# Order of the work between the pair loop and the first tile, and of the last stores, in a Hyena filter with a maxout FFN

## The chip, the core and the metric

The kernel runs on one core of a Trainium2 chip: TensorE (PE, matrix products into PSUM), VectorE (DVE), ScalarE (ACT), GpSimd (POOL) and SyncE (SP), each with its own instruction stream, and 16 DMA engines that serve transfers issued by SP, ACT and POOL. The metric is the device time of one execution in microseconds. Several executions give a median; one more is taken with the hardware profiler, and its trace gives the times inside.

## The reference

A long convolution (done with a Fourier transform) of u = x v with a filter that comes from a small MLP, a product with x, and a maxout FFN on the result:

```python
def _attn_ref(x, v, pos_emb, w1, w2):            # x, v: (4, 12544, 128)
    h_mlp = np.maximum(pos_emb @ w1, 0.0) @ w2
    window = np.exp(-0.01 * np.arange(S))[:, None]
    h_filt = h_mlp * window
    u = x * v
    L = 2 * S
    Uf = np.fft.rfft(u, n=L, axis=1)
    Hf = np.fft.rfft(h_filt, n=L, axis=0)
    y = np.fft.irfft(Uf * Hf[None, :, :], n=L, axis=1)[:, :S, :]
    return x * y

def _moe_ref(x, w1, w2, w3, w_out):              # x: (50176, 128), w1..w3: (128, 768)
    h = np.maximum(np.maximum(x @ w1, x @ w2), x @ w3)
    return h @ w_out
```

All arrays are float32.

## The kernel before

**The transform.** The 12544 positions of a batch entry are cut as 98 blocks (n) of 128 phases (p). The transform over n gives 90 frequencies, handled as 45 pairs (NK = 45); the transform over p, with its twiddle factors, is a product with a 128x128 matrix for each frequency. The input is taken in 32 units of 4 rows of 4 channels: a unit is loaded (`u_load`), multiplied (`u_mul`), turned with PE (`u_turn`), transformed over n (`u_products`) and written into `spec` in SBUF. `u_products` returns three further steps: `top`, a copy by ACT; `sums`, four DVE operations; `fours`, four more. `u_first` does all at once.

**The pair loop** (from line 1171) makes, for batch entry 0 and for each pair g: the filter's spectrum; the forward products `g_second`; the product with the spectrum (`g_re`, `g_im`); the sums `ab` of `g_unfold`; and the inverse products `g_third`, three pairs later. `g_third` copies its PSUM bank to `zs` with ACT, and SP stores `zs` to `zd` in HBM. The last pair's zs is copied besides to a small HBM tensor `ze` (two rows for each half c), by SP and by ACT. The matrices of `g_third` are loaded by `load_dir(s, 1)` on SP, three pairs ahead, into three buffers; the call stands behind that of `g_third`, so behind the store to `zd` on SP.

**The tiles.** A tile is 4 phases x 98 blocks, 392 positions; there are 32 for each batch entry. `t_load` reads its 90 rows from zd into `zt` (rows by frequency, halves c of 45 rows). For the first tile, POOL loads 44 rows of each half from zd, and SP the last row of each half from ze; POOL loads x for tiles 0 and 1 (`x_load`, four DMAs of 98 KB) ahead of zt. `t_sums` makes sum and difference of zt's halves. `t_last` multiplies them by a 90x98 table (32 matmuls over the four phases, s = 0 to 3), and DVE multiplies by x, which gives `gt`. Then come the FFN's steps. `up` makes hid = max(relu(gt (w2 - w1)), gt (w3 - w1)) for 128 of the 768 columns: two products into banks of `hps` (three banks, in turn), a relu by ACT, a max by DVE. `down` multiplies by w_out and adds up in a bank of `ops`, together with gt times `lin` = w1 w_out.

**The passage** (lines 1209 to 1234 and 1267 to 1284), by hand, between loop and tiles: units 0 and 1 of batch entry 1 (`u_first`), the last two `g_third` (pairs 43 and 44), six `folding` steps that make `lin` (a transpose of 128 columns of w1, an ACT copy `w1t`, a product into `pl`), the turning of units 4 and 5, the products of units 2, 3 and 4, and the first tile's sums and `t_last`. Each step needs PSUM banks: `cps` has three of tag "cv", `gps` two (g0, g1), `sps` two of tag "h" and one, `pl`. When the loop's pools are closed, the tiles' pools take the same banks.

**The rest.** While the tiles of one batch entry run, a planner (`conv_steps`) spreads the next entry's transform over them. The last entry's tiles are taken in pairs with an FFN of fewer products (`products`, `ORDER`); its results c11, c12, c21 and c22 are quarters of the output of two tiles (first digit: tile; second: half m of the output columns), kept in one buffer for each m, and `stored(m)` writes both of a buffer: for the last two tiles with one DMA on SP and one on ACT for each quarter. In the plan, c21 is followed by `stored(0)`, and c12, the last one, by `stored(1)`.

Each engine runs its instructions in the order in which they are written down here; the waits between engines are put in by the framework from the buffers read and written.

Of the kernel before, what the change touches and what calls it, by code (L numbers as in the profile page):

```python
# [16 lines left out]
P = 128  # L17
GC = 4
# [77 lines left out]
def kernel(  # L96
# [32 lines left out]
    zd = [dram.tile([N1, 2, 64, 256] if b == 0 else [N1, 2, 32, 2, 256], FP32, name=f"zd{b}")  # L129
          for b in range(B)]  # L130

    ze = dram.tile([2, 2, 2, 256], FP32, name="ze")

    f1_t, f1e_t, f1h_t, f4p_t, w_t, wq_t = tables(NB)
    f1_d = nc.inline_tensor(f1_t, name="f1_const").ap()
# [512 lines left out]
                                    op=op)  # L648
        abs_[g] = ab

    def g_third(g):
        w, ab = ws.pop((g, 1)), abs_.pop(g)
        ps = state["cv"][1].tile([P, 512], FP32, tag="cv", name="ps3")
        for k in range(2):
            for q in range(2):
                halves_mm(ps[:, (2 * k + q) * D:(2 * k + q + 1) * D], w[:, k, q, :],
                          ab[:, k, q, :], k == 0 and q == 0, True)
        if g < NK - 2:
            zs = state["cv"][0].tile([P, 2, 256], FP32, tag="z", name="zs", bufs=2)
        else:  # L660
            zs = lwp.tile([P, 2, 256], FP32, tag="w1", name="zs")
        nc.scalar.copy(zs[:].rearrange("p k f -> p (k f)"), ps[:])
        if g == NK - 1:
            for c in range(2):
                (nc.scalar if c else nc.sync).dma_start(ze[c], zs[64 * c:64 * c + 2])
        nc.sync.dma_start(
            zd[0][2 * g:2 * g + 2].rearrange("k c t f -> (c t) k f"), zs[:])

# [105 lines left out]
    def x_load(b, i, eng):  # L774
# [3 lines left out]
                          x[:, 4 * i:4 * i + 8, c, b, :])  # L778
        xTs[b, i], xTs[b, i + 1] = xT[:, 0], xT[:, 1]

    def t_load(b, i):
        if b == i == 0:
            x_load(b, i, nc.gpsimd)
        zt = hp.tile([N1, 2, 512], FP32, tag="zt", name="zt", bufs=2)
        for c in range(2):
            if b == 0:
                n = NK if i else NK - 1
                (nc.sync if i else nc.gpsimd).dma_start(
                    zt[NK * c:NK * c + n],
                    zd[b].rearrange("(g a) c t f -> g a c t f", a=2)[  # L790
                        0:n, :, c, 2 * i:2 * i + 2, :].rearrange("g a t f -> g a (t f)"))
                if i == 0:
                    nc.sync.dma_start(
                        zt[NK * c + n:NK * c + NK].rearrange("o a (t f) -> o a t f", t=2),
                        ze[c:c + 1].rearrange("o t a f -> o a t f"))
                continue
            q, j = divmod(i, NT // 2)
            for a in range(2):
                nc.sync.dma_start(
                    zt[NK * c:NK * c + NK, a].rearrange("g (t f) -> g t f", t=2),  # L800
                    zd[b].rearrange("(g a) c t q f -> g a c t q f", a=2)[
                        :, a, c ^ (a & q), 2 * j:2 * j + 2, q, :])
        zts[b, i] = zt[:, 0], zt[:, 1]
        if i % 2 == 0 and (b or i > 2):
            x_load(b, i, nc.gpsimd if 0 < i < NT - 2 and b < B - 1 else nc.sync)

# [94 lines left out]
    def products(b, i, h, X, Y):  # L901

        m1, m2 = lin[:, 0:64], lin[:, 64:128]
        first, second_ = gs[b, i], gs[b, i + 1]
        t = {}

        def new(name, bufs=1):
            return lp.tile([P, H2], FP32, tag=name, name=name, bufs=bufs)

        def mm(ps, w, rhs, start):  # L910
            for q in range(4):
                c, m = divmod(32 * q, 64)
                nc.tensor.matmul(ps[32 * q:32 * q + 32, 0:H2], w[:, m:m + 32],  # L913
                                 rhs[:, H2 * c:H2 * c + H2],
                                 start=start, stop=True, skip_group_check=True)

        def place(name):

            if name[0] != "c":
                t[name] = new(name)  # L920
                return t[name][:]
            n, m = int(name[1]) - 1, int(name[2]) - 1
            if m not in t:
                t[m] = lp.tile([P, 2, H2], FP32, tag="o", name="o", bufs=2)
            return t[m][:, n]

        def copied(name, ps):
            nc.scalar.copy(place(name), ps[:, 0:H2])

        def added(name, a, ps):  # L930
            nc.vector.tensor_tensor(out=place(name), in0=t[a][:], in1=ps[:, 0:H2], op=ALU.add)  # L931

        def stored(m):
            dst = outT.rearrange("d (p b n) -> d p b n", b=B, n=NB)
            for n in range(2):
                for c in range(2):
                    at = 4 * (i + n) + 2 * c
                    (nc.gpsimd if i < NT - 2 else (nc.sync, nc.scalar)[c]).dma_start(  # L938
                        dst[64 * m:64 * m + 64, at:at + 2, b, :],
                        t[m][64 * c:64 * c + 64, n].rearrange("d (q n) -> d q n", q=2))  # L940

        plan = (
            (X, "h11", wo_sb[:, 0:NC, 0:64], True, None, [(copied, "p1", X)], None),
            (Y, "s2", tw[:, 0], True, None, [(added, "u2", "p1", Y)], None),
            (X, "h12", wo_sb[:, NC:, 0:64], False, (m1, first), [(copied, "c11", X)], None),
            (Y, "s3", tw[:, 1], False, (m2, second_), [(added, "u3", "p1", Y)], None),
            (X, "h21", wo_sb[:, 0:NC, 64:128], True, None, [(added, "c22", "u3", X)], None),
            (Y, "h22", tw[:, 2], True, (linx[:], second_), [(added, "c21", "u3", Y)],
             (stored, 0)),
            (X, "h12", wo_sb[:, NC:, 64:128], False, (m2, first), [(added, "c12", "u2", X)],  # L950
             (stored, 1)),
        )
        out = []
        for ps, name, w, start, extra, then, store in plan:
            for j in range(NC):
                out.append([lambda ps=ps, name=name, w=w, start=start, j=j: mm(
                    ps, w[:, j, :], h[name, j][:], start and j == 0)])
            if extra:
                out.append([lambda ps=ps, extra=extra: mm(ps, extra[0], extra[1][:].rearrange("d p n -> d (p n)"), False)])
            out[-1] += [lambda a=a: a[0](*a[1:]) for a in then]  # L960
            out[-1].append(store)
        return out
# [19 lines left out]
    def load_dir(g, a):  # L982
        w = lwp.tile([P, 2, 2, P], FP32, tag=f"w{a}", name="wt")
        nc.sync.dma_start(w[:].rearrange("p k r m -> p (k r m)"), wt_d[g, :, a, :])
        return w
# [185 lines left out]
    for s in range(NK + 1):  # L1171
# [9 lines left out]
            s_filter(s - 1)  # L1181
        if s >= 3:
            ws[s - 3, 1] = wi.pop(s - 3)
            g_third(s - 3)
            if s < NK:
                wi[s] = load_dir(s, 1)
        ready = [g for g in {NK: (s - 2, s - 1)}.get(s, (s - 2,)) if 0 <= g and s <= NK]
        for g in {NK - 2: (s - 2, s - 1), NK - 1: (s - 1,), NK: (s - 1,)}.get(s, (s - 2,)):
            if 0 <= g and s <= NK:
# [19 lines left out]
    def one_bank(pool, tag):  # L1209
        return pool.tile([P, 512], FP32, tag=tag, name="ps1")[:]  # L1210

    g0, g1 = one_bank(gps, "g"), one_bank(gps, "g")
    u_first(0, (g0, g1), "x")
    ws[NK - 2, 1] = wi.pop(NK - 2)
    g_third(NK - 2)
    hb = sps.tile([P, 1024], FP32, tag="h", name="ps1")[:, 0:512]
    pl = sps.tile([P, 512], FP32, tag="pl", name="pl")
    u_first(1, (one_bank(cps, "cv"), hb), "x")
    fb = one_bank(cps, "cv")
    folds = iter((fb,))  # L1220
    folding(0)
    ws[NK - 1, 1] = wi.pop(NK - 1)
    g_third(NK - 1)
    folds = itertools.cycle((one_bank(cps, "cv"), fb))
    turn_banks = iter((g0, g1))
    state["turn"] = lambda: next(turn_banks)
    for f in range(1, NF):
        folding(f)
        if f in (2, 3):
            u_turn(f + 2)  # L1230
    while folded:
        folded.pop(0)()
    nc.scalar.copy(lin[:], pl[:, 0:D])
# [30 lines left out]
    for n, (b, i) in enumerate(tiles[:LAST]):  # L1264
        if i == 0:
            plan, pairs_from = plans[b]
        if n == 0:
            t_load(*tiles[0])
            t_load(*tiles[1])
            nc.gpsimd.dma_start(sign_t[:], sign_d)  # L1270
            second_ = u_products(2, (next(hbanks), next(hbanks)))
            second_[0]()
            first_ = ops.tile([D, 512], FP32, tag="ops", name="ps1")
            spare = state["bank"]()
            third = u_products(3)
            fourth = u_products(4, (spare[:, 0:512], spare[:, 512:1024]), "xs")
            t_sums(tiles[0], nc.vector)
            third[0]()
            second_[1]()
            fourth[0]()  # L1280
            t_last(tiles[0], first_)
            second_[2]()
            for fn in fourth[1:]:
                fn()
        for f in range(NF):

            if i < NT - 2:
# [7 lines left out]
            if f == 4 and n + 1 == LAST:  # L1295
                t_sums(tiles[n + 2], nc.vector)
            h = up((b, i), f)
            if n == 0 and f in (1, 2):
                third[f]()
            for a in range(2):  # L1300
                if f == plan[i][a]:
                    t_sums(tiles[n + 1],
# [109 lines left out]
```

## Time and profile before

| | |
|---|---|
| median of 3 runs | 2207.62 us (2207.11 to 2208.13) |
| the profiled execution | 2205.64 us, span 2203.9 us |
| PE busy | 2186.5 us (99%) |
| DVE, ACT, POOL busy | 1533.7, 1211.4, 1183.3 us |
| granted TensorE clock | 0.999 |
| DMA | 411.62 MB, mean 187 GB/s |

The span runs from the first to the last instruction of the profiled execution; the execution's own time has a little more around it. PE is busy nearly always, so what matters is where it is not. The page's chain of waits, followed back from the last instruction, says the same:

```profile
PE 93%; DVE 2%; POOL 2%; issue 1%; DMA 0%; ACT 0%; POOLq 0%; ACTq 0%; DVEq 0%
PE hps L169 46%; PE ops L169 20%; PE ops L913 6%; PE cps L169 4%; PE cps L549 3%; PE cps L451 3%; PE ps L178 3%; PE cps L559 3%; PE ps L169 2%; POOL xt L640 1%; PE last L169 1%; DVE ab L647 1%; PE ps L393 1%; DVE xs L639 1%; POOL specH L640 1%
```

Line 169 is the helper that issues a matmul in column blocks; the tile names (hps, ops, ps, cps, last) tell the stages apart. Between 0 and 110 us the filter and the spectra are made, from 110 to about 273 the pair loop runs, then the passage, then the tiles.

### The profile page before, as it was taken

How to read it: one execution, taken by the hardware profiler on the slowest of the kernel's cores; microseconds unless marked ns; L12 is line 12 of the kernel's file. 1: busy time of each engine (PE TensorE's matmuls, PEld its weight loads, DVE VectorE, ACT ScalarE, POOL GpSimd, SP SyncE). 2: the span in 40 equal slices, each digit the busy share in tenths (PEclk: the TensorE clock that was granted, in tenths of full speed). 3: DMA queues.
4: the chain of work that ended last, by engine and by line, in shares of the span. 5: the costliest groups of instructions: out<-in, count | busy, mean ns of one | idle time of the engine just before them, and what ended most of it. 6: DMA issues, size and time to landing. Idle time of an engine off the chain costs nothing.

```text
span 2203.9 us, 77207 instructions
## 1 busy us (share of the span) xinstructions
PE 2186.5 (99%) x31655; PEld 1258.5 (57%) x31655; DVE 1533.7 (70%) x3292; ACT 1211.4 (55%) x2223; POOL 1183.3 (54%) x1580
## 2 busy tenths in 40 slices
PE   9999999999999999999999999999999999999998
PEld 8988855555555555555555455555555545555565
DVE  5688966678888766668888766668878745454443
ACT  3699845466666555466666555456666522222222
POOL 1166568545544667535455566534545326666665
PEclk9999999999999999999999999999999999999999
DMA  8789999879999899789999899879999622222221
GB/s 200 184 262 318 302 181 206 170 196 247 248 245 246 209 189 178 155 193 243 245 245 251 212 193 175 171 172 244 242 251 241 179 75 59 65 71 69 59 59 24
DMA packets 491270, 411.62 MB, mean 187 GB/s; under 512 B 289379, under 2 KB 407901, under 8 KB 490917
## 3 DMA queue, kind: packets, MB, share of 16 engines
q1 hardware_dynamic: 443495, 274.33, 57.5%
q0 software_dynamic: 45936, 130.43, 20.9%
q8 instruction: 249, 4.08, 0.8%
q10 hardware_dynamic: 1486, 1.93, 0.4%
q14 instruction: 104, 0.85, 0.1%
HBM read 262.85 MB, written 84.68 MB: 158 GB/s over the span
## 4 chain that ended last, share of the span: by engine, by line
PE 93%; DVE 2%; POOL 2%; issue 1%; DMA 0%; ACT 0%; POOLq 0%; ACTq 0%; DVEq 0%
PE hps L169 46%; PE ops L169 20%; PE ops L913 6%; PE cps L169 4%; PE cps L549 3%; PE cps L451 3%; PE ps L178 3%; PE cps L559 3%; PE ps L169 2%; POOL xt L640 1%; PE last L169 1%; DVE ab L647 1%; PE ps L393 1%; DVE xs L639 1%; POOL specH L640 1%
## 5 line engine op out<-in xcount | busy, mean ns | idle before, releaser
L169 PE MATMUL hps<-gt,w_sb 128*64 128x392 f32 (+1 forms) x7672 | 1151.8, 494 | 1.8 <-DVE hid L852 1.0
L849 ACT ACTIVATE hid<-hps 128x392 f32<-128x392 f32 x768 | 382.4, 498 | 745.2 <-PE hps L169 726.9
L169 PEld LDWEIGHTS hps<-gt,w_sb 128*64 128x64 f32 (+1 forms) x7672 | 413.7, 126 | 454.5 <-issue 415.9
L852 DVE TENSOR_TENSOR hid<-hid,hps 128x392 f32<-128x392 f32 x768 | 428.5, 558 | 339.9 <-PE hps L169 321.4
L169 PE MATMUL ops<-hid,wo_sb 128*64 128x392 f32 x2304 | 476.8, 492 | 0.0
L601 POOL TENSOR_TENSOR cb<-cb,xs 128x512 f32<-128x512 f32 x135 | 178.2, 1320 | 358.3 <-DVE xs L598 349.8
L169 PEld LDWEIGHTS ops<-hid,wo_sb 128*64 128x64 f32 x2304 | 165.7, 137 | 213.5 <-issue 213.5
L574 DVE TENSOR_TENSOR cb<-cps,eo 128x512 f32<-128x512 f32 (+1 forms) x288 | 175.2, 650 | 78.0 <-ACT eo L571 76.9
L867 POOL DMA_DIRECT2D out_dram<-ot x96 | 77.1, 803 | 263.6 <-ACT ot L865 247.3
L589 ACT ACTIVATE xs<-cb 32x512 f32<-32x512 f32 x270 | 169.5, 628 | 21.9 <-DVE cb L574 13.1
L590 ACT COPY xs<-cb 32x512 f32<-32x512 f32 x270 | 166.3, 616 | 3.1
L605 DVE TENSOR_TENSOR xs<-cb 128x256 f32<-128x256 f32 x270 | 148.3, 598 | 7.3 <-POOL cb L601 7.3
L431 ACT COPY uT<-turned 113x512 uint16<-113x512 uint16 x180 | 125.9, 770 | 1.9 <-DMA turned<-planes 1.7
L388 POOL TENSOR_TENSOR ut<-ut 128x392 f32<-128x392 f32 x90 | 92.8, 1032 | 43.1 <-DMA ut<-in_vr_dram 42.9
L582 POOL DMA_DIRECT2D zd<-cb x135 | 93.8, 695 | 39.9 <-DVE cb L574 36.8
L169 PEld LDWEIGHTS cps<-f4p,even 90*64 90x64 f32 x1552 | 87.2, 138 | 35.9 <-issue 33.1
L777 POOL DMA_DIRECT2D xT<-in_x_dram x172 | 101.4, 605 | 4.6 <-DVE ab L647 3.1
L473 DVE TENSOR_TENSOR low<-high,cps 128x180 f32<-128x180 f32 x186 | 54.7, 336 | 68.9 <-ACT high L463 68.9
L938 POOL DMA_DIRECT2D out_dram<-o x120 | 72.6, 610 | 45.6 <-DVE o L931 44.5
L169 PE MATMUL cps<-f4p,zt 90*64 90x49 f32 x1552 | 95.9, 222 | 0.0
L415 POOL COPY planes<-ut 128x392 uint16<-128x392 uint16 x180 | 94.9, 561 | 0.0
L169 PE MATMUL cps<-f4p,even 90*64 90x49 f32 x1552 | 94.6, 220 | 0.0
(173 smaller groups left out, 3306.1 us busy)
## 6 DMA issues: line engine op xcount, KB each, us to landing
ht<-hd SPq DMA_DIRECT2D x264, 256.0 KB, 6.8
wt<-wq_const POOLq DMA_DIRECT2D x144, 256.0 KB, 5.6
zd<-cb POOLq DMA_DIRECT2D x135, 256.0 KB, 5.1
zt<-zd SPq DMA_DIRECT2D x384, 90.0 KB, 3.8
sq<-spec SPq DMA_DIRECT2D x528, 64.0 KB, 5.9
ut<-in_xr_dram SPq DMA_DIRECT2D x128, 196.0 KB, 4.0
ut<-in_vr_dram SPq DMA_DIRECT2D x128, 196.0 KB, 4.3
wt<-wt_const SPq DMA_DIRECT2D x90, 256.0 KB, 5.1
```

Of the source, the lines that this page charges most:

```text
L169: nc.tensor.matmul(out[h:h + w], lhsT[:, h:h + w], rhs, start=start, stop=stop, skip_group_check=True)
L415: nc.gpsimd.tensor_copy(w[:, h, :, :, 0:HB], a[:].bitcast(U16).rearrange("p s (m e h) -> p h s e m", e=2, h=2)[:, h])
L431: nc.scalar.copy(uts[u][0:HR, 8 * (u % 2):8 * (u % 2) + 8].rearrange("n s r t -> n (s r t)").bitcast(U16).rearrange("n (s r t h) -> n h s ...
L574: nc.vector.tensor_tensor(out=cb[:, a, lo:hi], in0=ps[:, lo:hi], in1=eo[:, lo:hi], op=op)
L589: nc.scalar.mul(xs[at:at + 32], xt[at + 32:at + 64], -1.0)
L590: nc.scalar.copy(xs[at + 32:at + 64], xt[at:at + 32])
L601: nc.gpsimd.tensor_tensor(out=xts[g], in0=xts[g], in1=xs[:], op=ALU.add)
L605: nc.vector.tensor_tensor(out=ab[:, q], in0=y[:, 0], in1=y[:, 1], op=(ALU.subtract, ALU.add)[q])
L777: eng.dma_start(xT[c * NG:(c + 1) * NG].rearrange("d i p n -> d (i p) n"), x[:, 4 * i:4 * i + 8, c, b, :])
L849: nc.scalar.activation(h[:], pa[:, 0:N], Relu)
L852: nc.vector.tensor_tensor(out=h[:], in0=h[:], in1=pb[:, 0:N], op=ALU.max)
L913: nc.tensor.matmul(ps[32 * q:32 * q + 32, 0:H2], w[:, m:m + 32], rhs[:, H2 * c:H2 * c + H2], start=start, stop=True, skip_group_check=True)
```

## The change

It has these parts:

- `g_third` takes a function that it calls between the copy to zs and the stores; the loop passes it `load_dir(s, 1)`, so this load stands ahead of the store to zd on SP.
- ze holds two pairs: the zs of pairs 43 and 44 are both copied to it, and the first tile's POOL loads take 43 rows of each half instead of 44, the loads from ze two rows.
- x of tile 0 goes into a buffer of the units' pool (`x0`, four DMAs of half the size), issued at the start of the passage; x of tile 1 alone is loaded behind zt (four DMAs again).
- The passage is reordered: `u_turn(4)` stands ahead of the last `g_third`, `u_turn(5)` behind it; units' turns and folds take their banks in turn from cps; unit 1 takes both banks of tag "h"; unit 2 is made from start to end before the last three folds, in g0 and g1, where before its products and steps stood around the first tile's sums.
- The first tile's sums are made in two halves of 256 columns; unit 3's `sums` follows `t_last`, its `fours` and unit 4's steps follow the first three `up`.
- For the last two tiles each quarter is stored as soon as it is made: the order is c11, c22, c21, c12.

```diff
-    ze = dram.tile([2, 2, 2, 256], FP32, name="ze")
+    ze = dram.tile([2, 2, 2, 2, 256], FP32, name="ze")
...
-    def g_third(g):
+    def g_third(g, then=None):
...
         nc.scalar.copy(zs[:].rearrange("p k f -> p (k f)"), ps[:])
-        if g == NK - 1:
+        if then:
+            then()
+        if g >= NK - 2:
             for c in range(2):
-                (nc.scalar if c else nc.sync).dma_start(ze[c], zs[64 * c:64 * c + 2])
+                (nc.scalar if c else nc.sync).dma_start(
+                    ze[c, g - NK + 2].rearrange("a t f -> t a f"), zs[64 * c:64 * c + 2])
...
+    def x_one(xT, i):
+        for c in range(GC):
+            nc.gpsimd.dma_start(xT[c * NG:(c + 1) * NG], x[:, 4 * i:4 * i + 4, c, 0, :])
+
     def t_load(b, i):
-        if b == i == 0:
-            x_load(b, i, nc.gpsimd)
...
-                n = NK if i else NK - 1
+                n = NK if i else NK - 2
...
+        if b == i == 0:
+            xT = hp.tile([D, 2, 4, NB], FP32, tag="xT", name="xT", bufs=2)
+            x_one(xT[:, 1], 1)
+            xTs[0, 1] = xT[:, 1]
...
+        stores = [p[6] for p in plan]
+        if i == NT - 2:
+            for at, m, n in ((2, 0, 0), (4, 1, 1), (5, 0, 1), (6, 1, 0)):
+                stores[at] = stored, m, (n,)
...
-            g_third(s - 3)
-            if s < NK:
-                wi[s] = load_dir(s, 1)
+            g_third(s - 3, (lambda: wi.update({s: load_dir(s, 1)})) if s < NK else None)
...
+    x0 = inp.tile([P, 4, NB], FP32, tag="u0", name="x0")
+    x_one(x0, 0)
+    xTs[0, 0] = x0[:]
     g0, g1 = one_bank(gps, "g"), one_bank(gps, "g")
+    state["turn"] = lambda: one_bank(cps, "cv")
+    folds = (one_bank(cps, "cv") for _ in range(NF))
     u_first(0, (g0, g1), "x")
     ws[NK - 2, 1] = wi.pop(NK - 2)
     g_third(NK - 2)
-    hb = sps.tile([P, 1024], FP32, tag="h", name="ps1")[:, 0:512]
+    hb = sps.tile([P, 1024], FP32, tag="h", name="ps1")
     pl = sps.tile([P, 512], FP32, tag="pl", name="pl")
-    u_first(1, (one_bank(cps, "cv"), hb), "x")
-    fb = one_bank(cps, "cv")
-    folds = iter((fb,))
+    u_first(1, (hb[:, 0:512], hb[:, 512:1024]), "x")
     folding(0)
+    u_turn(4)
     ws[NK - 1, 1] = wi.pop(NK - 1)
     g_third(NK - 1)
-    folds = itertools.cycle((one_bank(cps, "cv"), fb))
-    turn_banks = iter((g0, g1))
-    state["turn"] = lambda: next(turn_banks)
-    for f in range(1, NF):
+    folding(1)
+    u_turn(5)
+    folding(2)
+    second_ = u_products(2, (g0, g1), "x")
+    second_[0]()
+    for fn in second_[1:]:
+        fn()
+    for f in range(3, NF):
         folding(f)
-        if f in (2, 3):
-            u_turn(f + 2)
...
-            second_ = u_products(2, (next(hbanks), next(hbanks)))
-            second_[0]()
-            first_ = ops.tile([D, 512], FP32, tag="ops", name="ps1")
-            spare = state["bank"]()
-            third = u_products(3)
-            fourth = u_products(4, (spare[:, 0:512], spare[:, 512:1024]), "xs")
-            t_sums(tiles[0], nc.vector)
+            third, fourth = u_products(3), u_products(4, None, "xs")
             third[0]()
-            second_[1]()
             fourth[0]()
-            t_last(tiles[0], first_)
-            second_[2]()
-            for fn in fourth[1:]:
-                fn()
+            z0, z1 = zts[tiles[0]]
+            even = hp.tile([N1, 512], FP32, tag="even", name="even", bufs=2)
+            for h in range(2):
+                at = slice(256 * h, 256 * h + 256)
+                for out, op in ((even, ALU.add), (z1, ALU.subtract)):
+                    nc.vector.tensor_tensor(out=out[:, at], in0=z0[:, at], in1=z1[:, at], op=op)
+            zts[tiles[0]] = even[:], z1
+            t_last(tiles[0], ops.tile([D, 512], FP32, tag="ops", name="ps1"))
+            third[1]()
...
-            if n == 0 and f in (1, 2):
-                third[f]()
+            if n == 0 and f < 3:
+                (third[2], fourth[1], fourth[2])[f]()
```

More of the change, by code (lines that the diff above doesn't have):

```diff
@@ L793, in t_load @@
                     nc.sync.dma_start(
-                        zt[NK * c + n:NK * c + NK].rearrange("o a (t f) -> o a t f", t=2),
-                        ze[c:c + 1].rearrange("o t a f -> o a t f"))
+                        zt[NK * c + n:NK * c + NK],
+                        ze[c].rearrange("g a t f -> g a (t f)"))
                 continue
@@ L931, in added, with stored @@
             nc.vector.tensor_tensor(out=place(name), in0=t[a][:], in1=ps[:, 0:H2], op=ALU.add)
-        def stored(m):
+        def stored(m, ns=(0, 1)):
             dst = outT.rearrange("d (p b n) -> d p b n", b=B, n=NB)
-            for n in range(2):
+            for n in ns:
                 for c in range(2):
@@ L953, in products @@
         out = []
-        for ps, name, w, start, extra, then, store in plan:
+        stores = [p[6] for p in plan]
+        if i == NT - 2:
+            for at, m, n in ((2, 0, 0), (4, 1, 1), (5, 0, 1), (6, 1, 0)):
+                stores[at] = stored, m, (n,)
+        for (ps, name, w, start, extra, then, _), store in zip(plan, stores):
             for j in range(NC):
```

## The prediction

> **What bounds the kernel now.** I read first the table by stages, which says where TensorE (PE) is not busy, then PE's timeline where it is not, then the chain of waits there, and last the end of the program. In the table each row is a stretch, its length, and the busy time of PE, weight loads, VectorE (DVE), ScalarE (ACT) and GpSimd (POOL).
>
> ```profile
> 255.00:270.00 15.00, 13.56 (x304) 11.56 (x300) 13.81 (x33) 14.14 (x27) 5.49 (x9) 1.00 0.85 246
> 270.00:284.00 14.00, 10.51 (x240) 8.12 (x233) 9.23 (x29) 6.83 (x17) 4.39 (x8) 1.00 0.63 177
> 284.00:300.00 16.00, 14.97 (x144) 7.08 (x146) 11.32 (x35) 4.01 (x9) 12.48 (x20) 1.00 0.86 168
> 300.00:760.00 460.00, 459.73 (x5420) 239.04 (x5418) 346.23 (x728) 281.35 (x512) 253.67 (x346) 1.00 0.99 220
> 2190.00:2204.00 14.00, 8.04 (x180) 5.68 (x172) 2.42 (x7) 0.82 (x2) 5.87 (x7) 0.88 0.14 30
> ```
>
> From 300 us on PE lacks 0.27 us in 460, and over the whole span 2203.9 - 2186.5 = 17.4 us. So an edit of order, with PE's work unchanged, can win only in the passage (255 to 300 us, where PE lacks 6.0 us) and at the end (6.0 us). PE's timeline of the passage, with the gap ahead of a group in brackets:
>
> ```profile
> 270.52 0.33 PE L1099 MATMUL ps<-eye,w_sb 128*128 128x128 f32 x1
> 271.85 1.09 PE L169 MATMUL ps<-ab,wt 128*64 128x128 f32 x16 [1.00 <-DMA wt<-wt_const]
> 273.62 0.44 PE L1099 MATMUL ps<-eye,w_sb 128*128 128x128 f32 x2 [0.68 <-ACT zs L662]
> ...
> 281.56 0.32 PE L169 MATMUL ps<-f4p,even 90*64 90x49 f32 x4 [0.50 <-issue]
> 282.23 0.32 PE L169 MATMUL ps<-f4p,zt 90*64 90x49 f32 x4 [0.35 <-DVE zt L818]
> ...
> 283.92 2.85 PE L169 MATMUL hps<-gt,w_sb 128*64 128x392 f32 x16 [0.67 <-DVE gt L839]
> 287.80 1.54 PE L169 MATMUL hps<-gt,w_sb 128*64 128x392 f32 x8 [1.03 <-DVE hid L852]
> ```
>
> With a gap of 0.30 at 278.36 these are 4.53 us. They don't add up as a gain: the chain of waits (start, length, work) shows what the first tile waits for.
>
> ```profile
> 270.46 4.16 DMA zd<-zs
> 275.23 0.67 POOL zt L788
> 275.90 4.79 DMA zt<-zd
> 280.76 0.70 DVE even L818
> 281.49 0.70 DVE zt L818
> ```
>
> Rows of z go out to zd, come back as zt at 280.69, and the sums on DVE release PE at 282.23. What PE does faster before that only lengthens its wait, unless zt comes earlier too.
>
> **zt's landing.** It has two halves. The POOL loads were issued at 275.23, 0.61 us after pair 43's store had landed (274.62). Now they need only pairs up to 42, whose store landed at 273.92: issue at 274.53, the second 0.67 later. Before, four loads of x (98 KB each, the last landed at 279.08) ran ahead of them in the same queue; now x0's four go out from 269.3 (after POOL's stores of 268.22, 1.04 us; 4 x 0.59) and the other four behind zt. So the second load takes between 3.9 us (the least of the five zt loads here) and 4.79 as now: it lands at 279.1 to 280.0. The other half is the two loads out of ze. The completion records put the later one, issued on SP at 276.73, at 280.51, 3.78 us for 4 KB; the write of ze before it took 2.3 (273.59 to 275.86). It was hidden by 0.17 us alone. It now carries two pairs' rows and starts no sooner: the last products (271.85) need ab, which DVE ends at 270.91 + 0.76 = 271.67, and ACT copies unit 4's rows (1.17 us, from about 271.9) ahead of zs, at 273.1 against 272.98. So it lands 2.3 to 3.8 us after 276.8, at 279.1 to 280.6. I take 279.9 for the later of the two, nearer to the rows of this very load: 0.8 us won (0.1 to 1.6).
>
> **Sums in halves.** Now two operations of 0.69 us end 1.49 after the landing. Halves are 256 wide: a pair like it (ab, 128x256, two in 0.76) suggests a first pair ready 0.65 us earlier and the second 0.1 later. The 16 products on the first half take 4 x 0.12 = 0.47, so PE waits some 0.25 for the second: 0.4 us won (0.2 to 0.65).
>
> **PE's own work.** It is unchanged, and must be over by the time the sums are. Turning unit 4 (1.0 us at 274.26) fills the gap at 270.85. The weights that ended this gap (issued 266.51, behind the zd store that waits for ACT) can go at 264.5, when the products that held their buffer end, and land in 5.2 us (the loop's median) at 269.7. From 271.8 on, 281.06 - 271.85 = 9.2 us of groups and gaps, less 1.0 for the turn and 0.98 of gaps, plus some 0.5 of new waits (unit 3's products wait for the lin copy and for DVE's sums of unit 2), end at about 279.6. That is before the sums (280.7): no further cost; were the new waits above 1.5 us they would count.
>
> **Behind the first tile.** The 1.03 at 287.80 is PE waiting for a hid that DVE takes up at 287.20, after units 2 and 4. Unit 2 (8 operations, 2.2 us) moves to where DVE idles (4.46 us before 280.76); of unit 3 only the first four stand ahead of hid, and the other steps alternate with the next hids. From gt: 1.35 for the four (288.14 to 289.49 now), then hid ends 2.0 us after gt, while PE needs its bank after two rounds, 2.85 us. I take the whole 1.0 (0.5 to 1.03, if ACT or DVE slips).
>
> **The end.** The last sum ends at 2198.49; two stores each are then issued:
>
> ```profile
> 2198.13 0.36 DVE L931 TENSOR_TENSOR o<-u,ops 128x196 f32<-128x196 f32 x1 [0.97 <-PE ops L913]
> 2198.51 1.25 SPq L938 DMA_DIRECT2D out_dram<-o  x2
> 2198.52 1.52 ACTq L938 DMA_DIRECT2D out_dram<-o  x2
> ```
>
> One of each pair (c22, summed at 2195.89) goes out before, so the last issue starts 0.65 us sooner (2199.16 and 2199.19 become 2198.51): 0.65 won, 0.3 if the final write is slow anyhow, 0.85 if ACT's second issue (0.85) counts whole.
>
> **Edits at nothing.** Four more POOL issues (2.3 us) lie in POOL's idle 6.73 us before 283.85; without that cover tile 1's sums would be late. The issues of pair 43's ze rows (ACT 0.23, SP 0.30) delay unit 1's copy by 0.2, which DVE, busy until 272.07, doesn't see. Behind SP's new waits for ze stand tile 1's loads, which wait for pair 44's store anyway. x0's buffer is free at gt (282), and the unit that reuses it is loaded at 286. In the pair loop the w1 load passes the zd store on SP: PE is busy 60.00 of 60 us (140 to 200), so nothing can be won, and the load is issued while SP waits for zs.
>
> **Sum:** 0.8 + 0.4 + 1.0 + 0.65 = 2.85 us, bounds 1.1 and 4.1. The profiled execution took 2205.64 us around its span of 2203.9; I expect 2201.05 and 2202.8. The median shown is 1.98 higher: 2207.62 - 2.85 = 2204.8, own range 2203.5 to 2206.5.
>
> **Rivals.** A: the stall behind the first tile stays (DVE has as much to do there, and runs in order): against it stands the 2.0 against 2.85 above. 1.85 us remain: 2205.8. B: all PE gaps go. 1.00 + 0.68 + 0.30 + 0.50 + 0.35 + 1.03 = 3.86 and 0.85 at the end are 4.7: 2202.9. ze's 3.78 us for 4 KB speaks against it. C, slower: the loads of 43 rows, once 44, run on one DMA engine. The shortest packet of a row (4096 bytes) took 0.159 us, one beside other traffic 0.25; the first began 1.96 after issue. From 274.5, 1.96 + 43 x 0.159 to 43 x 0.25 ends at 283.3 to 287.2, which is 2.6 to 6.5 later than 280.69; less 2.05 (halves, hid, end) it is 0.6 to 4.5 slower, middle 2210.2. It decides from a landing after 282.7. Against it: the window's loads at the start, also from POOL and of 41 rows, went out as 13 packets of three rows and one of two, eight of them starting between 4.17 and 4.45 us, so on many engines. [...] D: in the loop a weight load ahead of the zd store holds the store back (issues took up to 2.57 us), zs comes free late, and ACT (58.25 of 60 us busy) stalls; 0.1 us in each of 42 pairs would give 4.2 less 2.85, 2209.0. Against it: zd lands in 4.9 us (median), and its buffer, one of two, is wanted again only 6.2 us after the issue (two pairs of 3.42 us, less 0.6).
>
> **How the numbers follow.** Forecast 0.62, A 0.19, B 0.08, C 0.06, D 0.05. Runs of this kernel tell 0.2% (4.4 us) from no change: faster is below 2203.2, slower above 2212.0. Faster: B and a part of the forecast's edge, 0.12. Slower: C's upper end, D with a larger stall, and what I haven't seen, 0.05. The rest 0.83. The range, 2203.2 to 2207.4, leaves out B, C and D and little of the rest.
>
> **What would show it.** Right: the last products of the loop at about 271.8 behind the turn; POOL's zt issue near 274.5; four sums from about 280.0; the first hps products near 282.7 (283.92 less 1.2) and no gap behind them; four stores' issues apart at the end. Wrong: sums starting at 280.7 or later (ze), a gap for hid, zt loads beyond 282.7 (C), or any gap of PE within the loop (D).

## The result, and the profile after

The changed kernel takes 2217.27 us (median of 6 runs, 2215.52 to 2218.49), the kernel before 2207.78 beside it (6 runs, 2207.11 to 2208.29): ratio 1.0043, 95% interval 1.003 to 1.0056. It is slower by 9.5 us; 2204.8 was forecast, within 2203.2 to 2207.4. The profiled execution after took 2215.52 us around a span of 2213.7.

The table by stages of the kernel after, in the columns shown of before, has the loss in one stage:

```profile
255.00:270.00 15.00, 13.64 (x304) 11.77 (x304) 13.86 (x34) 14.51 (x27) 5.96 (x11) 1.00 0.87 263
270.00:284.00 14.00, 10.07 (x214) 7.35 (x208) 8.96 (x30) 7.03 (x17) 8.01 (x11) 0.98 0.68 151
284.00:300.00 16.00, 9.21 (x64) 4.75 (x64) 7.54 (x20) 1.49 (x3) 3.79 (x5) 0.59 0.45 105
300.00:760.00 460.00, 459.75 (x5448) 239.34 (x5446) 347.80 (x736) 280.41 (x510) 257.37 (x351) 1.00 0.98 217
```

From 284 to 300 PE does 64 instructions where it did 144, and the third number from the end, the granted clock, is 0.59 instead of 1.00. PE's timeline of that stretch:

```profile
279.38 1.48 PE L451 MATMUL cps<-f1e,uT 49*64 49x90 f32 x64 [0.47 <-DVE spec L487]
290.12 0.46 PE L169 MATMUL ps<-f4p,even 90*64 90x49 f32 x4 [9.25 <-POOL zt L827]
290.53 0.46 PE L169 MATMUL ps<-f4p,zt 90*64 90x49 f32 x4
290.78 0.42 PE L169 MATMUL ps<-f4p,even 90*64 90x49 f32 x4
...
292.93 6.22 PE L169 MATMUL hps<-gt,w_sb 128*64 128x392 f32 x24 [0.67 <-DVE gt L848]
298.98 0.82 PE L169 MATMUL ops<-gt,lin 128*64 128x392 f32 x4
```

PE waits 9.25 us, and then works slowly: a group of four takes 0.42 to 0.46 us, the last 24 before `lin` 6.22. The wait is put down to POOL's sums of tile 1, which came last by the records; what PE needs are DVE's sums of tile 0, and those wait for a DMA (DVE's timeline, then the DMA issues of the page: number, size, median us from issue to landing):

```profile
278.65 0.59 DVE L487 TENSOR_TENSOR spec<-ps,low 128x180 f32<-128x180 f32 x2
288.97 1.04 DVE L1296 TENSOR_TENSOR even<-zt 90x256 f32<-90x256 f32 x1 [9.74 <-DMA zt<-zd]
```

```profile
zt<-zd POOLq DMA_DIRECT2D x2, 172.0 KB, 13.8
xT<-in_x_dram POOLq DMA_DIRECT2D x4, 49.0 KB, 11.5
```

Before, the first of these lines read

```profile
zt<-zd POOLq DMA_DIRECT2D x2, 176.0 KB, 4.9
```

So POOL's two loads of 43 rows landed at 288.21 and 288.89 instead of 280.69, though they were issued sooner (273.91 and 275.50), and the loads of x behind them came late too. In the completion records 15 of the 16 engines report for the first load, and 14 for the second, 2 to 3 us after the issue's end; the rest follow 9 to 10 us later. The packets say the same: 86 rows of 4096 bytes between 276.79 and 288.04, 0.25 us apart for each load (0.165 each at the end), and 1290 packets of 8 bytes, 15 for each row; before there were 40 in all. So one engine moved all rows of each load: rival C.

A ruler for what follows is the passage's length, from the start of pair 42's copy zs, where the loop is taken to end, to the weight load of the first `ops<-gt,lin`: 20.54 us before, 29.81 after. (Two of the expectations name pair 43 in its place; their numbers are of this stretch.) Of the 9.9 us between the two spans, it holds 9.3; the loop was 0.5 longer, the rest 0.1.

### The profile page after: what moved, and what is told of

Same layout as the page of the kernel before. It is cut to its first block, busy times and chain, and to the rows that moved or that the text cites. A ratio compares the mean times of both kernels' runs of the same rounds, so it can differ in the third digit from the quotient of the medians.

```text
span 2213.7 us, 77215 instructions
## 1 busy us (share of the span) xinstructions
PE 2189.9 (99%) x31655; PEld 1296.4 (59%) x31655; DVE 1534.3 (69%) x3294; ACT 1213.6 (55%) x2223; POOL 1190.2 (54%) x1584
## 4 chain that ended last, share of the span: by engine, by line
PE 92%; POOL 3%; DVE 2%; issue 2%; DMA 1%; ACT 0%; SPq 0%; POOLq 0%; ACTq 0%; DVEq 0%
PE hps L169 46%; PE ops L169 20%; PE ops L922 6%; PE cps L169 4%; PE cps L549 3%; PE cps L451 3%; PE ps L178 3%; PE cps L559 3%; POOL xt L640 1%; PE ps L169 1%; PE last L169 1%; DVE ab L647 1%; DVE xs L639 1%; PE ps L393 1%; POOL specH L640 1%
## 5 line engine op out<-in xcount | busy, mean ns | idle before, releaser
L169 PEld LDWEIGHTS hps<-gt,w_sb 128*64 128x64 f32 (+1 forms) x7672 | 433.3, 126 | 438.5 <-issue 384.8
L605 DVE TENSOR_TENSOR xs<-cb 128x256 f32<-128x256 f32 x270 | 148.3, 597 | 7.3 <-POOL cb L601 7.3
```

Of the source, the lines that this page charges most:

```text
L169: nc.tensor.matmul(out[h:h + w], lhsT[:, h:h + w], rhs, start=start, stop=stop, skip_group_check=True)
L605: nc.vector.tensor_tensor(out=ab[:, q], in0=y[:, 0], in1=y[:, 1], op=(ALU.subtract, ALU.add)[q])
```

## The experiments

The first runs ask whether the number of rows is the cause, or the crowd of transfers that the new order brings.

**e1: 44 rows again.** All else as in the kernel after; ze holds the last pair only.

```diff
-        if g >= NK - 2:
+        if g == NK - 1:
...
-                n = NK if i else NK - 2
+                n = NK if i else NK - 1
...
```

> The change with 44 rows in POOL's two loads of zt again, and with the last pair's rows alone in ze; all else as changed. Theory ROWS (a POOL load of 43 rows of two runs each is put on one DMA engine; 44 rows are not): the two loads are issued at 275 to 277 us and land within 3.9 to 5.2 us of their issue, by 281.5 at the latest; no PE gap above 2 us in the passage, granted clock 1.0 there; 2204 to 2207 us. Theory CROWD (the loads are late because x, ze and zd are now issued in another order around them): they still take over 10 us to land and the time stays within 2 us of 2217.

2206.61 us (11 runs; ratio 0.9995, 0.9986 to 1.0004). The loads of 44 rows land 3.4 us after the issue:

```profile
zt<-zd POOLq DMA_DIRECT2D x2, 176.0 KB, 3.4
```

PE waits 0.2 us for the sums behind them, the clock stays at 1.0, and the passage is 17.96 us. They were issued later than expected, at 279.17 and 279.83, because the loop of this profile ended 3.6 us later than that of before.

**e2: 42 rows.** Three pairs go through ze.

```diff
...
-                n = NK if i else NK - 2
+                n = NK if i else NK - 3
```

> The change with 42 rows in POOL's two loads and three pairs' rows in ze. ROWS: 42 rows spread as well, the loads are issued near 273 us and land in 3.9 to 5.2 us, near 278; the ze loads then come last (279 to 281); 2203.5 to 2206.5 us. CROWD: within 2 us of 2217 (a ze that carries more would not help).

2205.57 us (11 runs; ratio 0.999, 0.9982 to 0.9999), passage 17.43.

```profile
zt<-zd POOLq DMA_DIRECT2D x2, 168.0 KB, 5.1
```

Fewer rows and more of them are both quick; of the counts tried, 43 alone is slow.

**e3: the kernel before with 43 rows** (two pairs through ze), no other part of the change.

```diff
...
-        if g == NK - 1:
+        if g >= NK - 2:
...
-                n = NK if i else NK - 1
+                n = NK if i else NK - 2
...
```

> The kernel before with nothing changed but 43 rows in POOL's two loads and the last two pairs' rows in ze. ROWS: the loads land 12 to 15 us after their issue, PE idles 8 to 11 us ahead of the first tile, and the time is 7 to 11 us above the kernel before. CROWD: within 2 us of the kernel before.

2219.53 us in one run, 12.0 above the kernel before, where 7 to 11 were expected. The loads take 13.1 us to land, PE waits 10.0 us ahead of the first tile, and the granted clock between 284 and 300 us is 0.62. So this part alone makes the loss; with the other parts it is 9.5 us.

**e4: 43 rows, each of one run.** Each POOL load is cut so that a row is one run of 2048 bytes, not two:

```diff
...
+                    for a in range(2):
+                        nc.gpsimd.dma_start(
+                            zt[NK * c:NK * c + n, a],
+                            zd[b].rearrange("(g a) c t f -> g a c t f", a=2)[
+                                0:n, a, c, 0:2, :].rearrange("g t f -> g (t f)"))
...
```

> The kernel after, 43 rows, but each of POOL's two zt loads cut into two, so that a row of a load is one run of 2048 bytes (four loads of 43 rows). If the number of rows alone decides (43 is prime): all of a load on one engine, the last of the four lands 9 us or more after its issue, PE waits 5 to 10 us ahead of the first tile's products, time 2213 to 2218. If the form with two runs in a row decides (the window's loads of 41 rows and one run went out on many engines): the packets start on many engines at once, landing 3.5 to 5.5 us after the issue, no wait of PE above 2 us, time 2205 to 2208.

2208.72 us in one run (2205 to 2208 expected), passage 21.30 because the clock fell (last section). The four loads land in 4.6 us, each as 14 times three rows and one row more.

```profile
zt<-zd POOLq DMA_DIRECT2D x4, 86.0 KB, 4.6
```

So the same 43 rows are spread when a row is one run, and half as long. The window's load of 41 rows, which I held against C, is of that form, and says nothing of rows of two runs.

**e6, e6b: 32 and 11 rows.** The whole change with its 43 rows; each of POOL's two loads is cut in two.

```diff
-                (nc.sync if i else nc.gpsimd).dma_start(
-                    zt[NK * c:NK * c + n],
+                for lo, hi in ((0, n),) if i else ((0, 32), (32, n)):
+                    (nc.sync if i else nc.gpsimd).dma_start(
+                        zt[NK * c + lo:NK * c + hi],
```

> The kernel after with its 43 rows from zd, but each of POOL's two loads cut into one of 32 rows and one of 11, in the same form of two runs for each row. If the number of rows decides how many engines move a load (43 has no divisor but itself): the last of the four lands 4 to 6 us after its issue and PE waits less than 2 us ahead of the first tile, passage 17 to 20 us where the clock stays at 1.0, up to 22 where it falls, 2205 to 2209 us. If it is the bytes or the crowd in the queue: landing 10 us or more, passage near 29, 2214 to 2219.

2204.08 us in one run, passage 17.91.

```profile
zt<-zd POOLq DMA_DIRECT2D x2, 128.0 KB, 4.0
zt<-zd POOLq DMA_DIRECT2D x2, 44.0 KB, 3.7
```

> e6 timed: the whole change with its 43 rows, the two POOL loads cut into 32 and 11 rows. Passage 2.6 us shorter than before, the end 0.1 longer, loop the same or up to 2 longer: 2205 to 2207 beside 2207.5 of before, ratio 0.9988 to 0.9997; all of the 9.5 us that the change lost come back. If LOOP theory holds, in the upper half of that; if the time has another cause beside the engine count, above 2208.

2205.61 us (11 runs; ratio 0.9993, 0.9984 to 1.0002; before 2207.27), passage 17.80. The 9.5 us come back, and some 1.7 more, which the interval doesn't part from none.

The packets of 8 bytes allow an estimate of how many engines moved a load. Suppose that k of the 16 that report for a load share its n rows evenly, and that each of the other 16 - k leaves one such packet in each round of rows, as 15 did for each row in the kernel after; then a load leaves n / k x (16 - k) of them. The traces have 1290 (after, e3, e9, e9b) for two loads of 43 rows, 40 (before, e1, e5, e8) for two of 44, 12 (e2, and e7, e10, e11, e14, e15, which have 42 rows too) for two of 42, and 10 (e6, e6b) for two of 32 and two of 11. That gives k = 1, 11, 14, and 16 and 11.

The landings go with this estimate: 43 rows of two runs took 13.8 us (after) and 13.1 (e3), 44 took 4.9 (before) and 3.4 (e1), 42 took 5.1 (e2), 32 and 11 took 4.0 and 3.7 (e6). Rows of one run went out otherwise (e4: 14 times three and one more, 4.6 us). Other counts of rows of two runs were not tried in these loads.

**e9, e9b: PE kept busy in its wait.** In the kernel after, extra products of `w_sb` go into the first tile's bank and are written over by it.

```diff
+            first_ = ops.tile([D, 512], FP32, tag="ops", name="ps1")
+            for _ in range(24):
+                halves_mm(first_[:, 0:N], w_sb[1][:, 0:P], w_sb[2][:, 0:N], True, True)
+            t_last(tiles[0], first_)
```

> The kernel after, 43 rows, with 48 more matmuls of 392 columns (0.178 us each, 8.5 us) on PE while it waits for the first tile's sums; their results are written over by the first tile's products. CLOCK theory (the idle time of 9 us brings the granted clock to 0.5 from 284 to 297 us, and work there takes twice as long): clock 1.0 throughout the passage, the 32 products of the first tile 0.29 us for each group of four (0.42 after), the first 24 of hps 4.2 us (6.2 after), passage 26 to 27 us (29.86 after), time 2213 to 2214.5. Other theory (these products are slow because of the transfers that run beside them, or because their operands come late): clock 1.0, but the same 6.2 us and a passage of 29 to 30.

I had mis-sized it: a product of 392 columns makes two instructions (96 in the trace, where I expected 48), so the extra work took 16 us, not 8.5, and hid the wait and more (2220.04 us in one run). But behind it the clock was 1.0 throughout. PE's timeline:

```profile
281.87 16.02 PE L169 MATMUL ps<-w_sb,w_sb 128*64 128x392 f32 x96
297.72 0.27 PE L169 MATMUL ps<-f4p,even 90*64 90x49 f32 x4
...
299.48 4.17 PE L169 MATMUL hps<-gt,w_sb 128*64 128x392 f32 x24 [0.67 <-DVE gt L848]
303.48 0.83 PE L169 MATMUL ops<-gt,lin 128*64 128x392 f32 x4
```

From the first tile's products to `lin` PE takes 5.76 us, and 8.86 in the kernel after (290.12 to 298.98): the fallen clock cost 3.1 us there, on top of the wait.

e9b has half the extra work:

```diff
-            for _ in range(24):
+            for _ in range(12):
```

> The kernel after, 43 rows, with half as much extra work on PE in its wait as in the run before this one: 48 products instead of 96, 0.167 us each, so 8.0 us in a wait of 9.3. CLOCK theory (what makes the work behind the wait slow is the granted clock, which falls because PE was idle): clock 1.0 in the whole passage, 24 products of hps in 4.17 us (6.22 after), from pair 43's copy zs to the first ops<-gt,lin 26.4 to 27.2 us (29.81 after; 20.54 before), and 2213 to 2215.5 us in all. Rival (the extra work lies in the way and costs as much as the clock gives): 29 to 30 us again.

2220.28 us in one run, passage 30.55: by its number the rival's, and a little more, but by another way. PE was busy until 290.8, and then waited twice for DVE's sums, which ran beside POOL's sums of tile 1 (DVE's timeline, then PE's):

```profile
290.82 0.70 DVE L1296 TENSOR_TENSOR even<-zt 90x256 f32<-90x256 f32 x1 [9.74 <-DMA zt<-zd]
291.55 1.37 DVE L1296 TENSOR_TENSOR zt<-zt 90x256 f32<-90x256 f32 x1
```

```profile
282.65 8.12 PE L169 MATMUL ps<-w_sb,w_sb 128*64 128x392 f32 x48
291.62 0.32 PE L169 MATMUL ps<-f4p,even 90*64 90x49 f32 x4 [0.85 <-POOL even L827]
292.98 0.43 PE L169 MATMUL ps<-f4p,zt 90*64 90x49 f32 x4 [1.03 <-DVE zt L1296]
```

After these gaps of 0.85 and 1.03 us the clock was 0.5 for 6.8 us. The same sums take 0.42 us each where POOL is not at its own (e7).

**e5: before with the last stores by quarters**, nothing else of the change.

```diff
...
+        if i == NT - 2:
+            for at, m, n in ((2, 0, 0), (4, 1, 1), (5, 0, 1), (6, 1, 0)):
+                stores[at] = stored, m, (n,)
...
```

> The kernel before with the last stores by quarters alone. The prediction's step: the last issue starts 0.65 us sooner and the end with it, 2207.1 us against 2207.75. Rival DRAIN: the last landing comes 0.6 us sooner after the last sum, but what follows it in the program's end (2.4 us in the trace of before, 3.5 in that of the change) takes the gain back: within 0.2 us of before.

2207.42 us (11 runs; ratio 0.9995, 0.9987 to 1.0004). From DVE's last sum, the last landing comes 2.39 us later instead of 3.00, as forecast; the span's end comes 5.38 later, against 5.37 before. What ends last is the drain, the instruction with which POOL closes its stream: it is 10.2 us long and ends 4.6 us after DVE's last sum in both, while SP reaches its own at 3.5 us before and at 2.9 here. In the kernel after and in e1, e2, e4, e6 and e7 the stores are as quick, but the drain is longer (10.7 us) and the end 5.87 to 5.90 us after DVE's last sum. In before, after and e10 (next) these are the drains, with the shortest, median and longest of them in ns, and the first and last start:

```profile
L1407 POOLq DRAIN  x3: 46/98/10173, 2192.9 to 2203.6; - x3
L1422 POOLq DRAIN  x3: 46/98/10703, 2202.3 to 2213.5; - x3
L1424 POOLq DRAIN  x3: 46/98/8048, 2193.0 to 2201.7; - x3
```

**e10 and e11** ask what makes this drain long. Both start from e7 (below). In e10 SP stores six more tiles' results in POOL's place; in e11 the last six sums of POOL are made by DVE.

```diff
-                    (nc.gpsimd if i < NT - 2 else (nc.sync, nc.scalar)[c]).dma_start(
+                    (nc.gpsimd if i < NT - 8 else nc.sync if i < NT - 2 else (nc.sync, nc.scalar)[c]).dma_start(
```

```diff
...
-        sum_(h["h21", j], h["h21", j], h["h22", j], ALU.add)
+        sum_(h["h21", j], h["h21", j], h["h22", j], ALU.add, h.get("eng"))
...
-        sum_(h["h12", j], h["h12", j], h["s2", j], ALU.subtract)
+        sum_(h["h12", j], h["h12", j], h["s2", j], ALU.subtract, h.get("eng"))
...
-        h = {}
+        h = {"eng": nc.vector} if i == NT - 2 else {}
```

> The kernel of 42 rows with the old order on SP (e7), with the results of six more tiles stored by SP instead of POOL. It asks what sets the end of the program: in all runs so far the span ends 5.37 to 5.39 us after DVE's last sum where the passage is that of before, and 5.87 to 5.90 where it is the new one, whether the last stores go by halves or by quarters; POOL's closing drain (10.2 and 10.7 us) ends last, 2.0 to 2.5 us after SP's. Theory DMA (the drain is long because POOL's queue had transfers until late): from DVE's last sum to the end 3.4 to 4.2 us instead of 5.87, POOL's drain shorter than 9. Theory OPS (the drain ends a fixed time after POOL's last operation): 5.87 again.

> The kernel of 42 rows with the old order on SP (e7), with the last pair of tiles' last six sums on DVE instead of POOL, so that POOL's last operation ends some 6 us sooner. Theory OPS: from DVE's last sum to the end of the span 3.4 to 4.0 us instead of 5.87 (then SP's drain sets it). Theory DMA: 5.87 again, or no more than 0.5 less. Both: the passage as in e7, 17.8 us, and DVE, idle there, adds no wait of PE above 0.5 us.

e10: 2203.71 us in one run, the drain 8.05 us, the end 3.37 us after DVE's last sum. e11: 2204.56, the drain 9.8 us but begun 5.0 us earlier against DVE's last sum, the end 3.39 after the sum. Each theory's lever works by itself: the drain starts while POOL's last sums run, is shorter when POOL's last stores lie further back, and sets the end unless one of the two is moved. Then SP sets it, in e10 by 0.1 us. That the quarters count then was not tried without them.

**e7, e8: the order of load and store on SP in the loop.** e7 is e2 with the old order; e8 is the kernel before with the new one.

```diff
-            g_third(s - 3, (lambda: wi.update({s: load_dir(s, 1)})) if s < NK else None)
+            g_third(s - 3)
+            if s < NK:
+                wi[s] = load_dir(s, 1)
```

> The kernel after with 42 rows from zd and three pairs from ze, and the store to zd again ahead of the w1 load on SP (only in the pair loop). LOOP theory (the w1 load ahead of the store makes zs come free late, and ACT stalls): from the first zs copy to pair 42's 146.9 us as before (149.0 in the run of 42 rows with the new order, 149.8 in that of 44), ACT's wait for zd ahead of zs under 0.3 us in all (2.0 there), its wait for hd ahead of ht under 0.6 (1.4); passage from pair 43's products to the first ops<-gt,lin 17.5 us as there; so about 2 us less than that run, 2203.3 to 2204.3 beside a before of 2207.5, ratio 0.998 to 0.9988. NOISE theory (the loop's length differs by itself from execution to execution): 148 to 150 us again, time 2205.6.

> The kernel before with one part of the change alone: in the pair loop the w1 load ahead of the store to zd on SP. LOOP theory: the loop is 148.5 to 150 us long (146.9 before), ACT waits 0.4 to 2 us for zd and 1.4 to 3 us for hd, the passage stays at 20.6 us or gains up to 1.0 (the gap for the load of wt ahead of the last products goes): 2207.5 to 2210.0, ratio 1.000 to 1.001, clearly above what the store first gives. NOISE theory: loop 146.9, and with the gap of 1.0 gone 2206.5 to 2207.5.

The loop (first copy zs to pair 42's) was 147.2 us in e7 and 149.8 in e8, as the loop theory said. The times don't follow: e7 2206.6 (11 runs; ratio 0.9994, 0.9985 to 1.0002), no better than e2; e8 2207.51 (ratio 1.0002, 0.9993 to 1.0011). And e10, e11 and e6, profiled later, broke the pattern: 148.3 twice with the old order, 146.8 with the new.

**e14, e15: the two orders side by side.** e14 is e10 timed; e15 differs only in the loop's order.

> e10 timed: 42 rows, old order on SP in the loop, six more tiles' results stored by SP. From the profiles: passage 2.8 to 3.1 us shorter than before, from the first ops<-gt,lin to the end 1.9 shorter: 4.7 to 5.0 us less than before, ratio 0.9977 to 0.9979. If single profiles mislead (the timed runs of e7 gave 0.8 us where its profile gave 2.4): ratio 0.9985 to 0.999.

> e14 with one difference: in the pair loop the w1 load ahead of the zd store, as in after. LOOP theory: 1 to 2.5 us slower than e14 in the median of the timed runs, and a loop of 148 to 150 us. NOISE theory: within 0.7 us of e14.

e14: 2203.3 us (11 runs; ratio 0.9982, 0.9973 to 0.9991), 4.0 less than before, between its two forecasts. e15: 2203.78 (11 runs; ratio 0.998, 0.9972 to 0.9989). Within 0.5 us: by the time it is the noise theory's case. By the loop it is the other's: 149.4 us in e15's profile, 147.3 in e14's, and in e15 ACT waited 4.9 us, in seven waits, for the stores to zd ahead of its copies, in e14 not at all. Over all profiles these waits are 0 to 1.0 us with the old order (seven, mean 0.2) and 0 to 4.9 with the new (ten, mean 1.2); the loop is 146.9 to 148.3 us with the old (mean 147.5) and 146.8 to 149.8 with the new (mean 148.4). So the stall of rival D does occur. The means differ by 0.9 us, with a standard error of 0.4: a cost of some 1 us is likely in the loop, but the timed runs don't tell it from none. e14 is faster than both kernels of this study.

## Why the prediction was wrong

**The failed step is zt's landing:** "So the second load takes between 3.9 us (the least of the five zt loads here) and 4.79 as now". The second load took 13.4 us, because one engine moved all its 43 rows of two runs, some 0.25 us apart. Those five loads were all of 44 or 45 rows, and the least of them was SP's, so they bounded no load of 43. Rival C assumed just this, which no row of the trace of before had shown, and got 0.06, on the strength of one row, the window's 41 rows spread over many engines. That row has another form (one run for each row), and e4 shows that the form matters: 43 rows were spread too, and landed in 4.6 us, once a row was one run. With the forms told apart, no row of the trace spoke against C, and the 40 packets of 8 bytes, which by the estimate above fit 11 engines for 44 rows, stood in the trace of before.

**C's price was too low as well** (2210.2 in the middle, 2217.27 measured). The rows went 0.25 us apart, its upper bound; the issues took 1.59 us each, not 0.66; and the fallen clock, 3.1 us, was not in it. C was decided from a landing after 282.7; it came at 288.89.

**ze and the halves.** In e2, e6 and e7, where the rows go out in time, the load out of ze is the later of the two, as forecast (in e1 POOL's loads are, which wait for pair 43's store). In e7 DVE waits 0.74 us for it and starts the sums at 279.46, near the forecast 279.9, in part by luck: the load was issued at 277.66, not 276.8, and took 1.7 us, not 3.1. In the kernel after itself the loads out of ze had landed by 278.41, sooner than the forecast range. PE's own work, forecast to be over at 279.6, ends in e7 at 280.28, so PE waits for the sums 0.2 us at most:

```profile
278.87 1.48 PE L451 MATMUL cps<-f1e,uT 49*64 49x90 f32 x64 [0.47 <-DVE spec L487]
280.28 0.32 PE L169 MATMUL ps<-f4p,even 90*64 90x49 f32 x4
...
282.42 4.17 PE L169 MATMUL hps<-gt,w_sb 128*64 128x392 f32 x24 [0.67 <-DVE gt L848]
286.42 0.83 PE L169 MATMUL ops<-gt,lin 128*64 128x392 f32 x4
```

The first products of hps start at 282.42 in e7 (forecast 282.7), with the loop's end as before (268.31 against 268.30). How much of this the halves gave was not tried alone.

**Behind the first tile:** right. The 24 products run in one group, the gap of 1.03 us is gone in every run with the new order of units, and rival A falls. The three terms of the passage together were 2.2 us; in the runs with a quick zt and the clock at 1.0 (e1, e2, e6, e6b, e7, e10, e11, e14, e15) the passage is 17.4 to 18.0 us, 2.6 to 3.1 less than before.

**The end:** wrong, 0.65 forecast. The stores do land 0.6 sooner, but I took the last landing for the end of the span. POOL's closing drain ends later, so e5 gained nothing; with the whole change the end is even 0.5 us later, because this drain is 0.5 longer. Which part makes it so stayed open. The kernels with the short drain (10.2 us) issue 782 transfers from POOL, those with the long one (10.7) 786 or 788, and e10, with 8.0, 762; so the four more issues of x are a candidate, which no run tried alone.

**The loop:** "nothing can be won" held. That nothing is lost is doubtful: rival D's stall occurs, at some 1 us of the loop in the mean, not the 4.2 us of its price.

With the right numbers the sum for the kernel after is: passage -2.8 (as in e7), wait and clock +12.0 (29.81 less 17.78), end +0.5, loop +0.5 in that execution, 10.2 in all against 9.9 in the spans. Without the slow load the same terms leave a gain of 1.1 to 2.6 us (2.6 to 3.1 of the passage, less 0.5 at the end and up to 1 in the loop); e6b showed 1.7.

## What to carry to other kernels

Here a change of a load's shape was a change of how it was spread (44 rows landed in 3.4 to 4.9 us, 43 in 13.1 to 13.8). When an edit takes one row off a DMA, look for a row of the profile with the same form and row count, and where none exists, give the slow case its weight and cut the load into counts whose landing a run shows (here 32 and 11, 3.7 to 4.0 us, in place of 43). Ask of a saving at the end of a program what ends last there, including the engines' closing drains (here POOL's, of 10.2 us). Price a long wait of PE, or several short ones close together, with the slower work behind it (3.1 us here, behind a wait of 9.25).

## What the runs showed of the hardware

- **The clock fell after short gaps, too.** In the passage of e4 PE was never idle for more than 0.83 us at a time, and yet (table by stages, granted clock third from the end):

```profile
276.00:284.00 8.00, 6.51 (x140) 4.47 (x138) 5.93 (x21) 4.07 (x11) 4.67 (x9) 0.96 0.73 167
284.00:292.00 8.00, 7.33 (x52) 3.69 (x52) 4.71 (x15) 1.29 (x3) 2.83 (x3) 0.61 0.57 137
```

  The half-clock stretches in the passage lasted 3.41 us (e5, e8), 6.83 (e4, e9b) and 13.65 (after, e3), all multiples of 3.41. In after the clock's four changes lie 81, 4 and 561 times 3.413 us apart, in before its two 643 times. The kernel before has gaps of the same size (6.0 us in 45, the longest 1.03) and kept 1.0 there.

  What the traces show is PE's busy share in single stretches of 3.41 us, on the grid that the clock's own changes mark. Just ahead of the falls in the passage it was 59% (e8), 57% (e4, 279.94 to 283.35), 45% (e5, e9b), 24% (after) and nothing (e3); in before the lowest there is 70%. Over the 17 traces all 24 falls, 17 of them at the program's end, came behind a stretch of 59% or less, and of 10,915 stretches at full clock without a fall 6 were as low. So in these traces the falls go with the sum of the gaps within one stretch, not with the longest gap, and the grid lies otherwise from execution to execution (the clock's first change is at 5.83 us in before, at 6.97 in after): before and e5 share their passage, and the clock fell in one of them. This is read from the traces afterwards; no run was made to try it.
- **One profile is not a time.** Executions of the same kernel differ by 2 us in either direction (e2 2203.2 to 2208.0), and parts of them by 1 to 3: the loop took 147.3 and 148.3 us in e14 and e10, one kernel, and from the first `ops<-gt,lin` to the end e6 and e6b, one kernel too, took 1915.1 and 1917.9. Where the clock stays at 1.0, the passage's length repeats within 0.2 us (e6 and e6b, e10 and e14), and the end within 0.03; such stretches can be compared between profiles, sums of a whole span can't.
